# Decode attention: PV with p as an 8-column stationary and V moving 512 columns wide

## The chip, the core and the metric

One core of a Trainium2 chip runs the whole program. The metric is the device time in microseconds (us), median of several executions. All runs quoted below are undisturbed (fast). A ratio of two kernels is the mean time of one kernel's fast runs over that of the other's of the same rounds, so it is not quite the ratio of the medians that stand beside it; the interval with it is a 95% interval.

PE is the matmul engine, PEld its weight loads, DVE the vector engine, ACT the scalar engine, POOL a further engine that is all but idle here (2.4 us busy in before), SP the engine that issues the transfers. PSUM, in the code and the text, is where PE's results stand: the tiles `fold`, `otps`, `stps`, `qwps` and `yps` of the kernels, called banks here. The granted clock is the clock that PE was allowed, as a share of full speed, as the profile records it.

## The reference

Two independent halves, A and B, each a decode step of attention with one query token, 32 heads, 8192 cached tokens, head size 128, all bf16:

```
q = (x @ wq) per head                       # x: 1 x 512
scores = q . k_cache * 128**-0.5            # 32 heads x 8192
p = softmax(scores)
o = p @ v_cache                             # 32 heads x 128
y = concat(o) @ wo                          # 4096 x 512
```

K and V of both halves are 268 MB; everything else is small. The work is a long stream of transfers with little arithmetic on each byte.

## The kernel before

Heads are taken in pairs, 32 pairs over both halves. One pair's K, or V, is one 4 MB transfer into one of five slots of a ring, laid out with 64 partitions for each of the two heads and 128 tokens in each partition. For a pair j the engines do this:

- DVE multiplies K by q in place, in eight products M0 to M7.
- PE "folds" each half of the products over the head dimension: 16 matmuls against the identity, each moving 512 columns (fold 0 for M0 to M3, fold 1 for M4 to M7). DVE reduces the rest (R).
- The softmax goes over all engines: maxima on DVE (m1), a transpose on PE (tr), a maximum (m2), a broadcast on PE (bc), the exponents on ACT, their sum on PE (sum), the reciprocal on DVE (ri).
- PV multiplies p with V on PE. DVE scales the result into `ot` (o).

The parts that the change touches, with cuts marked by dots:

```python
def plan_PV(j):
    last = (j == NPR - 1)
    if not last:
        landed('PE', ('v', j))
    W('PE', c_e, e_val[j])                  # wait for the exponents
    if j >= 2:
        W('PE', c_o, o_val[j - 2])          # the PSUM bank is free
    t = kv(('v', j))
    ...
    def op(e, t0, t1):                      # TP = 128 tokens a partition
        for i in range(t0, t1):
            m = e.matmul(ot_ps[j % 2][:, 0:2], t[:, i, :], p2[:, j % 2, i, :],
                         start=(i == 0), stop=(i == TP - 1))
    ...
for j in range(NPR):                        # NPR = 32 pairs; c is j >= 1
    for i in range(4):
        plan_M(j, i)
    if j >= 2:
        plan_o(j - 2)
    if c:
        plan_R(j - 1, 1)
    plan_fold(j, 0)
    plan_M(j, 4)
    if c:
        plan_m1(j - 1)
        plan_tr(j - 1)
    plan_M(j, 5)
    if c:
        plan_m2(j - 1)
        plan_bc(j - 1)
        plan_exp(j - 1)
        plan_sum(j - 1)
    plan_M(j, 6)
    plan_M(j, 7)
    if c:
        plan_ri(j - 1)
    plan_fold(j, 1)
    plan_R(j, 0)
    if j < NPR - 1:
        if c:
            plan_PV(j - 1)
        if j == PPA + 1: ...plan_w(0, ...)  # half A: o rearranged for wo
        if j == PPA + 2: ...plan_y(0, ...)  # half A: y = o @ wo, 128 matmuls
        plan_w_ready(j - 2)                 # half B: o rearranged, in three blocks
...                                         # tail: the last pair, its PVs, y of B
```

Each engine runs its own list in the order in which these functions append to it. So in every pair PE does fold 0 of pair j, the small softmax products of pair j-1, fold 1 of pair j, PV of pair j-1.

In PV before, a 128x128 block of V is the stationary operand (a weight load) and the two columns of p move through it. For each of the 128 tokens of a partition there is one load and one 2-column matmul.

## Time and profile before

| | before |
|---|---|
| time, median of 3 | 683.4 us |
| span in the profile | 680.7 us |
| DMA | 90% or more in 39 of 40 slices, about 430 GB/s |
| mean granted PE clock | 0.79 |
| one pair, first fold matmul to the next pair's | 19.4 us in most pairs |

From the page: rows of the span in 40 slices (granted PE clock in tenths, mean busy share of the DMA engines in tenths, GB/s), then the chain of work that ended last by engine, then the costliest groups (busy us, mean ns of one, idle time before them and what ended it).

```profile
span 680.7 us, 12357 instructions
PEclk9998867877876867789867786967887668678885
DMA  9999999999999999999999999999999999999993
DMA 53%; PE 30%; DVE 12%; issue 3%; ACT 1%; ACTq 0%; DVEq 0%
L374 PE MATMUL fold<-ring,ident 128*128 128x512 bf16 x1024 | 320.5, 484 | 109.7 <-DVE ring L361 109.2
L361 DVE TENSOR_TENSOR ring<-ring,qbc 128x2048 bf16<-128x2048 bf16 x256 | 300.9, 1216 | 148.5 <-DMA ring<-in_A_k_cache_dram 84.9
L459 PE MATMUL otps<-p,ring 128*128 128x2 bf16 x4096 | 108.3, 163 | 1.5 <-issue 1.5
```

The transfers bound the kernel. Before its products DVE is idle 148 us in sum, waiting for K to land, and PE is idle because DVE is. The 8 MB of a pair at 430 GB/s take 19.5 us, and that is the pair's time.

From the timeline, PE's side of one early pair (start us, duration us, engine, line, operation; the row-sum product at 75.10 ends the softmax):

```profile
69.34 3.61 PE L374 MATMUL fold<-ring,ident 128*128 128x512 bf16 x16
72.79 0.27 PE L405 MATMUL stps<-ident_f,m 128*2 128x128 f32 x1
73.43 0.38 PE L415 MATMUL stps<-m,sel 2*128 2x1 f32 x2 [0.37 <-DVE m L410]
75.10 0.57 PE L436 MATMUL stps<-rowsum,ones_f 128*128 128x2 f32 x2 [1.29 <-ACT p L429]
75.70 5.02 PE L374 MATMUL fold<-ring,ident 128*128 128x512 bf16 x16
```

Here a fold takes 3.6 us or 5.0 us for the same 16 matmuls (in other pairs up to 6.6 us), 217 ns or up to 427 ns each. The granted clock is 1.00 over the first, 0.71 over the second and 0.54 over a fold of 6.6 us. Between the folds lies a gap of 2.8 us, in which PE waits for DVE and ACT. PV follows fold 1. The chain of waits (start us, us, what) has it at 3.21 us:

```profile
75.70 5.02 PE fold L374 x16
80.72 3.21 PE otps L459 x128
83.95 37.84 DMA ring<-in_A_k_cache_dram
```

3.21 us over 128 matmuls is 25 ns apiece, each with its own 128-column weight load; those of the last PVs, at a granted clock of 0.50, took 27 ns. The line at 83.95 is a K transfer that the end of PV let start, since it freed a slot of the ring. Three other transfers are still ahead of it and one lands every 9.7 us, so the rate of the transfers, and not the end of PV, sets when it lands, 37.84 us later.

### The profile page before, as it was taken

How to read it: one execution, taken by the hardware profiler on the slowest of the kernel's cores; microseconds unless marked ns; L12 is line 12 of the kernel's file. 1: busy time of each engine (PE TensorE's matmuls, PEld its weight loads, DVE VectorE, ACT ScalarE, POOL GpSimd, SP SyncE). 2: the span in 40 equal slices, each digit the busy share in tenths (PEclk: the TensorE clock that was granted, in tenths of full speed). 3: DMA queues.
4: the chain of work that ended last, by engine and by line, in shares of the span. 5: the costliest groups of instructions: out<-in, count | busy, mean ns of one | idle time of the engine just before them, and what ended most of it. 6: DMA issues, size and time to landing. Idle time of an engine off the chain costs nothing.

```text
span 680.7 us, 12357 instructions
## 1 busy us (share of the span) xinstructions
PE 479.8 (70%) x5660; PEld 264.9 (39%) x5660; DVE 377.8 (56%) x513; ACT 42.5 (6%) x169; POOL 2.4 (0%) x16
## 2 busy tenths in 40 slices
PE   0487877767688767856777576857768768667775
PEld 0133533434343434433433352534434234334445
DVE  4158556655555665555556526656555557463650
ACT  0110000000000000000000000000000001000000
POOL 1000000000000000000000000000000000000000
PEclk9998867877876867789867786967887668678885
DMA  9999999999999999999999999999999999999993
GB/s 370 431 430 431 431 433 429 429 430 430 427 435 433 428 430 432 430 426 430 431 430 429 431 430 430 428 405 432 429 432 432 428 426 430 430 430 433 422 415 131
DMA packets 11684, 286.01 MB, mean 420 GB/s; under 512 B 1776, under 2 KB 2288, under 8 KB 2672
## 3 DMA queue, kind: packets, MB, share of 16 engines
q1 hardware_dynamic: 11344, 285.22, 97.9%
q8 instruction: 44, 0.72, 0.4%
q14 instruction: 8, 0.07, 0.0%
q10 hardware_dynamic: 288, 0.00, 0.0%
HBM read 285.21 MB, written 0.00 MB: 419 GB/s over the span
## 4 chain that ended last, share of the span: by engine, by line
DMA 53%; PE 30%; DVE 12%; issue 3%; ACT 1%; ACTq 0%; DVEq 0%
DMA ring<-in_B_k_cache_dram 27%; DMA ring<-in_A_k_cache_dram 22%; PE fold L374 19%; DVE ring L361 11%; PE otps L459 7%; DMA xT<-in_B_x_dram 3%; PE qwps L333 2%; PE yps L537 1%; ACT qbc L340 1%; DVE m L410 1%; ACT p L429 0%; PE stps L436 0%; PE stps L405 0%; DVE wt L504 0%; PE stps L415 0%
## 5 line engine op out<-in xcount | busy, mean ns | idle before, releaser
L374 PE MATMUL fold<-ring,ident 128*128 128x512 bf16 x1024 | 320.5, 484 | 109.7 <-DVE ring L361 109.2
L361 DVE TENSOR_TENSOR ring<-ring,qbc 128x2048 bf16<-128x2048 bf16 x256 | 300.9, 1216 | 148.5 <-DMA ring<-in_A_k_cache_dram 84.9
L374 PEld LDWEIGHTS fold<-ring,ident 128*128 128x128 bf16 x1024 | 117.3, 120 | 287.8 <-issue 117.5
L459 PEld LDWEIGHTS otps<-p,ring 128*128 128x128 bf16 x4096 | 108.3, 97 | 8.7 <-issue 1.6
L459 PE MATMUL otps<-p,ring 128*128 128x2 bf16 x4096 | 108.3, 163 | 1.5 <-issue 1.5
L387 DVE TENSOR_REDUCE s_sb<-fold 128x64 f32<-128x512 f32 x64 | 43.1, 674 | 10.7 <-PE fold L374 10.3
L410 DVE TENSOR_REDUCE m<-stps 2x1 f32<-2x128 f32 x32 | 8.9, 279 | 69.8 <-PE stps L405 69.8
L436 PE MATMUL stps<-rowsum,ones_f 128*128 128x2 f32 x64 | 13.6, 282 | 41.5 <-ACT p L429 41.5
L421 ACT COPY nb<-stps 128x1 f32<-128x1 f32 x32 | 5.1, 159 | 580.3 <-PE stps L415 580.3
L333 PE MATMUL qwps<-ring,xsel 128*128 128x512 bf16 x64 | 16.7, 408 | 29.2 <-DVE xsel L226 24.3
L429 ACT ACTIVATE p<-s_sb,nb 64x128 bf16<-64x128 f32 x64 | 27.9, 436 | 2.1 <-ACT nb L421 0.3
L436 PEld LDWEIGHTS stps<-rowsum,ones_f 128*128 128x128 f32 x64 | 10.8, 211 | 44.2 <-ACT p L429 44.2
L333 PEld LDWEIGHTS qwps<-ring,xsel 128*128 128x128 bf16 x64 | 6.0, 103 | 39.4 <-issue 27.2
L415 PE MATMUL stps<-m,sel 2*128 2x1 f32 x64 | 12.3, 259 | 11.5 <-DVE m L410 11.5
L415 PEld LDWEIGHTS stps<-m,sel 2*128 2x128 f32 x64 | 9.6, 186 | 24.0 <-DVE m L410 24.0
L397 DVE TENSOR_REDUCE m<-s_sb 64x1 f32<-64x128 f32 x64 | 17.7, 277 | 1.0
L504 DVE TENSOR_TENSOR wt<-qwps,hmask 128x512 f32<-128x512 f32 (+3 forms) x5 | 2.2, 440 | 24.6 <-PE qwps L497 24.5
L429 ACT ACTIVATION_READ_ACCUMULATOR p<-s_sb,nb 64x1 f32 x64 | 11.7, 182 | 0.0
L475 DVE TENSOR_TENSOR ot<-otps,rinv 128x2 bf16<-128x2 f32 x32 | 4.9, 154 | 11.8 <-PE otps L459 11.8
L537 PE MATMUL yps<-w_bf,ring 128*128 128x1 bf16 x240 | 8.7, 172 | 1.9 <-issue 1.9
L537 PEld LDWEIGHTS yps<-w_bf,ring 128*128 128x128 bf16 x240 | 8.6, 118 | 1.9 <-issue 1.9
L405 PE MATMUL stps<-ident_f,m 128*2 128x128 f32 x32 | 8.8, 275 | 0.0
(30 smaller groups left out, 34.4 us busy)
## 6 DMA issues: line engine op xcount, KB each, us to landing
ring<-in_A_k_cache_dram SPq DMA_DIRECT2D x16, 4096.0 KB, 37.1
ring<-in_A_v_cache_dram SPq DMA_DIRECT2D x16, 4096.0 KB, 31.0
ring<-in_B_k_cache_dram SPq DMA_DIRECT2D x16, 4096.0 KB, 37.8
ring<-in_B_v_cache_dram SPq DMA_DIRECT2D x15, 4096.0 KB, 31.9
ring<-in_A_wq_dram SPq DMA_DIRECT2D x1, 4096.0 KB, 12.5
ring<-in_B_wq_dram SPq DMA_DIRECT2D x1, 4096.0 KB, 21.9
ring<-in_A_wo_dram SPq DMA_DIRECT2D x1, 4096.0 KB, 36.5
ring<-in_B_wo_dram SPq DMA_DIRECT2D x1, 2048.0 KB, 20.2
```

Of the source, the lines that this page charges most:

```text
L333: m = e.matmul(qw_ps[:, :].rearrange("p (j d) -> p j d", d=Dh), xsel[:, a, c, par, :], wq[:, c, 4 * g:4 * g + 4, par, :], start=(i == 0), ...
L361: m_val[(j, i)] = INC('DVE', c_m, lambda e: e.tensor_tensor(t, t, qbc[:, a, jj:jj + 1, :].broadcast_to([P, CH, Dh]), ALU.mult))
L374: m = e.matmul(fold_ps[h][:, :].rearrange("p (t e) -> p t e", e=FE), ident[:], t[:, h * HT:(h + 1) * HT, c * FE:(c + 1) * FE], start=(c == ...
L387: r_val[(j, h)] = INC('DVE', c_r, lambda e: e.tensor_reduce(s_sb[:, j % 2, h * HT:(h + 1) * HT], fold_ps[h][:, :].rearrange("p (t e) -> p ...
L397: m1_val[j] = INC('DVE', c_m1, lambda e, h=h, q0=q0, q1=q1: e.tensor_reduce(m1[q0:q1, j % 2, h:h + 1], s_sb[q0:q1, j % 2, :], AX.X, ALU.max))
L405: tr_val[j] = INC('PE', c_tr, lambda e: e.transpose(st_ps[j % 2][0:2, 0:P], m1[:, j % 2, :], ident_f[:]))
L410: m2_val[j] = INC('DVE', c_m2, lambda e: e.tensor_reduce(m2[0:2, j % 2:j % 2 + 1], st_ps[j % 2][0:2, 0:P], AX.X, ALU.max))
L415: bc_val[j] = INC('PE', c_bc, lambda e: e.matmul(st_ps[j % 2][:, P:P + 1], sel2[:], m2[0:2, j % 2:j % 2 + 1], start=True, stop=True))
L429: e_val[j] = INC('ACT', c_e, lambda e, h=h, q0=q0, q1=q1: e.activation(p2[q0:q1, j % 2, :, h], s_sb[q0:q1, j % 2, :], AF.Exp, bias=nb[q0:q ...
L436: s_val[j] = INC('PE', c_s, lambda e: e.matmul(st_ps[j % 2][:, P + 2:P + 4], ones_f[:], rowsum[:, j % 2, :], start=True, stop=True))
L459: m = e.matmul(ot_ps[j % 2][:, 0:2], t[:, i, :], p2[:, j % 2, i, :], start=(i == 0), stop=(i == TP - 1))
L537: m = e.matmul(y_ps[:, b:b + 1], wo[:, h0 + i, :, b], src[:, a, h0 + i:h0 + i + 1], start=(first and i == 0 and b == 0), stop=(lastblk and ...
```

## The change

The intent: the 4096 weight loads of PV look wasteful, each 128 columns for two columns of output. The change turns the product round. Four tokens of p for both heads are an 8-column stationary, and V moves through it, four tokens times 128 values, 512 columns wide: 32 matmuls a pair instead of 128. The result is an 8x512 block of which only the four 2x128 "diagonal" blocks (token with its own token) are wanted. ACT copies the block out of PSUM, and four small fp32 matmuls add the diagonal blocks and turn them back into two columns. The last two pairs keep the old PV.

The core of the diff; further lines make the tile `o8`, two semaphores, a wait of the transpose on the output multiply, and let PV wait for ACT's copy where it waited for the output multiply:

```diff
+            def wide(e):
+                for i in range(0, TP, TB):
+                    m = e.matmul(ot_ps[j % 2][0:2 * TB, :],
+                                 p2[:, j % 2, i:i + TB, :].rearrange("p t h -> p (t h)"),
+                                 t[:, i:i + TB, :].rearrange("p t d -> p (t d)"),
+                                 start=(i == 0), stop=(i == TP - TB))
+                m.then_inc(c_pv.sem, 1)
+            if j < NWIDE:
+                OP('PE', wide)
 ...
+                cp_val[j] = INC('ACT', c_cp, lambda e: e.copy(
+                    o8[:, j % 2, :], ot_ps[j % 2][0:2 * TB, :]))
 ...
+        def plan_ot(j):
+            W('PE', c_cp, cp_val[j])
+            W('PE', c_ri, ri_val[j])
+            v = ot_val[j] = c_ot.bump()
+
+            def op(e):
+                for i in range(TB):
+                    m = e.matmul(st_ps[j % 2][:, OC:OC + 2], o8[:, j % 2, i * Dh:(i + 1) * Dh],
+                                 ident_f[0:2 * TB, 2 * i:2 * i + 2],
+                                 start=(i == 0), stop=(i == TB - 1))
+                m.then_inc(c_ot.sem, 1)
+            OP('PE', op)
 ...
             for i in range(4):
                 plan_M(j, i)
-            if j >= 2:
-                plan_o(j - 2)
             if c:
                 plan_R(j - 1, 1)
             plan_fold(j, 0)
+            if j >= 2:
+                plan_ot(j - 2)
             plan_M(j, 4)
+            if j >= 2:
+                plan_o(j - 2)
             if c:
                 plan_m1(j - 1)
                 plan_tr(j - 1)
```

The fp32 products stand behind fold 0 on PE, and the output multiply that waits for them stands ahead of the maxima on DVE.

## The prediction

> **What bounds it now.** The page shows the DMA engines 90% or more busy in 39 of 40 slices at about 430 GB/s. A pair of heads brings 8 MB of K and V, so a pair costs 19.5 us of transfer; 32 pairs, wq and wo fill the span of 680.7 us. DMA leads the chain of waits (53%). PE is not far behind. From the timeline, one pair costs PE: fold 0 (16 matmuls 128x512, 3.5 us at full clock, 5.0 to 5.3 at half), a gap of 2.8 us for maximum, exponent and sum, fold 1 (3.6 to 5.3), and PV, 128 loads with 2-wide matmuls in 3.2 to 3.4 us at either clock. That is 13 to 17 us: PV is hidden.
>
> **What the change does.**
> 1. PV becomes 32 matmuls, each streaming 512 columns. The fold takes 217 ns each at full clock and 427 ns at half: estimate 6.9 us, or up to 13.7, for 3.3 us. PE gains +3.6 us a pair at best.
> 2. New: one ACT copy 8x512, about 0.6 us, hidden under fold 0; four fp32 matmuls with 128-column loads. The row-sum product shows two loads of 0.15 us, so about 1.2 us.
> 3. Order. The output multiply on DVE now comes after those fp32 matmuls, which come after fold 0, ahead of the maximum and of product 5. Now they follow serially: fp32 1.2, multiply 0.2, two maxima 0.6, product 5 1.2, then 2.6 as before to fold 1. PE's gap in a pair grows from 2.8 to about 5.8 us.
>
> **The new pair.** 3.5 + 5.8 + 3.5 + 6.9 = 19.7 us at full clock throughout: no slack against 19.5. [...] the clock records here show just 0.5 and 1.0, in multiples of 3.41 us. In this trace a window followed by full clock had about 6.5 or more 512-wide matmuls (40% of it streaming), and narrow PV hardly counted. A gap of 5.8 us always contains a window under that, so fold 1 starts at half clock and loses 1 to 2.5 us. Wide PV should count as activity, so it and fold 0 run warm. I estimate 20.5 to 22.5 us a pair, about 21.7: this loop bounds, DMA waits for slots.
>
> **Sum.** Fold 0 of pair 2 starts at 69.3 us, about 73 after. 29 pairs at 21.7 = 629; wo work of half A, now exposed, about 10; the tail from the last fold 0, about 32 as now (last two PVs unchanged); 2 us from span to time. I say 744.
>
> **Time: 744 us, 8 in 10 within 712 to 775. Faster by over 2%: 0.02; within 2%: 0.06; slower: 0.92.**
>
> **What would show it.** DMA busy digits drop to 8, rate near 385 GB/s; "DVE waits for K" nearly gone; chain mostly PE fold and PV instead of DMA; fold 0 near 217 ns a matmul, fold 1 partly 427; PV 6.9 us; mean clock up to about 0.85; fold starts 20.5 to 22.5 us apart.
>
> **What would make it wrong.** If an 8-column stationary does not count as activity, PV runs at half clock: 27 us a pair, over 880 us. If the gap is near 4.5 us, or the windows lock favourably (six are 20.48 us), about 710. If the fp32 matmuls overlap well, it stays DMA-bound, within 2%.

The sum: 73 + 629 + 10 + 32 + 2 = 746, stated as 744.

## The result, and the profile after

The changed kernel takes 777.1 us (775.6 to 781.3, four runs), before 683.3 us (682.4 to 684.3, four runs). The ratio is 1.138 (1.134 to 1.143). The direction and nearly all of the mechanism were as predicted; the time lies 2 us above the range and 33 us above the point.

The same lines of the page of after:

```profile
span 775.3 us, 7136 instructions
PEclk9999988988988988889988787988998869988786
DMA  9999999999999989899989598999998959989540
PE 77%; DVE 13%; ACT 4%; DMA 3%; issue 2%; DVEq 0%; ACTq 0%
L376 PE MATMUL fold<-ring,ident 128*128 128x512 bf16 x1024 | 303.0, 463 | 24.3 <-DVE ring L363 23.9
L363 DVE TENSOR_TENSOR ring<-ring,qbc 128x2048 bf16<-128x2048 bf16 x256 | 300.6, 1215 | 10.2 <-DMA ring<-in_A_k_cache_dram 9.2
L479 PE MATMUL otps<-ring,p 128*8 128x512 bf16 x960 | 212.1, 379 | 0.0
L525 DVE TENSOR_TENSOR ot<-stps,rinv 128x2 bf16<-128x2 f32 x30 | 4.8, 160 | 272.4 <-PE stps L510 272.4
```

DMA fell from 53% of the chain to 3%, and PE rose from 30% to 77%. DVE no longer waits for K (10 us in sum instead of 148). It waits 272 us for the fp32 products, 9 us in each pair. PE, with the steps of DVE and ACT between its two folds, has become the loop that everything else waits for. The mean clock rose to 0.86: wide PV runs at a granted clock of 1.00 in every pair (219 ns a matmul), and the regular fold 0 behind it takes 3.6 us where before has 5.6 us in the mean.

PE's side of one regular pair in the timeline of after (the four fp32 products show as x8):

```profile
312.99 3.63 PE L376 MATMUL fold<-ring,ident 128*128 128x512 bf16 x16
316.55 1.05 PE L510 MATMUL stps<-ident_f,o 8*128 8x2 f32 x8
318.42 0.27 PE L408 MATMUL stps<-ident_f,m 128*2 128x128 f32 x1 [0.82 <-DVE m L399]
319.87 0.38 PE L418 MATMUL stps<-m,sel 2*128 2x1 f32 x2 [1.18 <-DVE m L413]
321.54 0.59 PE L439 MATMUL stps<-rowsum,ones_f 128*128 128x2 f32 x2 [1.29 <-ACT p L432]
322.14 6.58 PE L376 MATMUL fold<-ring,ident 128*128 128x512 bf16 x16
```

And the chain of waits goes on from there without a wait for anybody but PE:

```profile
322.14 6.58 PE fold L376 x16
328.72 7.00 PE otps L479 x32
335.72 3.56 PE fold L376 x16
```

This pair is 3.6 (fold 0) + 5.5 (gap) + 6.6 (fold 1, here almost all at half clock) + 7.0 (PV). Over the regular pairs the mean is 21.81 us, with fold 1 at 5.7 us in the mean. PV's 32 matmuls at 219 ns cost 7.00 us where 128 small ones cost 3.21: the loads that the change removed had been cheaper than the columns that it moves.

The granted clock of fold 1 can be followed in time. The table below cuts the timeline of after into stretches of 3.4 us (for each engine busy us and number of instructions; then the granted clock, the DMA share, GB/s):

```profile
314.50:317.90 3.40, 3.10 (x18) 1.75 (x16) 0.19 (x2) 0.00 (x0) 0.00 (x0) 1.00 1.07 463
317.90:321.30 3.40, 0.65 (x3) 0.37 (x3) 3.34 (x6) 0.96 (x4) 0.00 (x0) 1.00 0.98 424
321.30:324.80 3.50, 3.25 (x9) 1.49 (x10) 3.42 (x5) 0.18 (x2) 0.00 (x0) 0.51 0.84 365
324.80:328.20 3.40, 3.40 (x10) 1.16 (x9) 2.67 (x3) 0.00 (x0) 0.00 (x0) 0.51 0.65 280
328.20:331.60 3.40, 3.40 (x17) 1.25 (x16) 1.82 (x2) 0.00 (x0) 0.00 (x0) 1.00 0.56 154
```

The second stretch lies in the gap; PE is busy 0.65 us of it, and the clock is halved in the third (0.51). The third has about six matmuls of fold 1 at half clock, and the fourth is halved too (0.51). The clock records of before and after hold only 0.5 and 1.0, and all but the last of each trace's entries (92 and 72) last 3.41 us or a whole multiple of it. "Window" below means one such 3.41 us of the record.

### The profile page after: what moved, and what is told of

Read it like the earlier page. It is cut to its first block, busy times and chain, and to the rows that moved or that the text cites. A ratio compares the mean times of both kernels' runs of the same rounds, so it can differ in the third digit from the quotient of the medians.

```text
span 775.3 us, 7136 instructions
## 1 busy us (share of the span) xinstructions
PE 614.3 (79%) x3020; PEld 274.8 (35%) x3020; DVE 379.0 (49%) x513; ACT 59.7 (8%) x199; POOL 2.4 (0%) x16
## 4 chain that ended last, share of the span: by engine, by line
PE 77%; DVE 13%; ACT 4%; DMA 3%; issue 2%; DVEq 0%; ACTq 0%
PE fold L376 38%; PE otps L479 27%; DVE ring L363 9%; PE stps L510 4%; DMA xT<-in_B_x_dram 3%; ACT p L432 3%; PE qwps L335 2%; PE stps L439 2%; DVE m L399 2%; PE stps L418 2%; PE yps L587 1%; PE otps L472 1%; DVE m L413 1%; DVE ot L525 1%; ACT nb L424 1%
## 5 line engine op out<-in xcount | busy, mean ns | idle before, releaser
L376 PE MATMUL fold<-ring,ident 128*128 128x512 bf16 x1024 | 303.0, 463 | 24.3 <-DVE ring L363 23.9
L363 DVE TENSOR_TENSOR ring<-ring,qbc 128x2048 bf16<-128x2048 bf16 x256 | 300.6, 1215 | 10.2 <-DMA ring<-in_A_k_cache_dram 9.2
L479 PE MATMUL otps<-ring,p 128*8 128x512 bf16 x960 | 212.1, 379 | 0.0
L376 PEld LDWEIGHTS fold<-ring,ident 128*128 128x128 bf16 x1024 | 112.9, 115 | 198.2 <-issue 106.0
L525 DVE TENSOR_TENSOR ot<-stps,rinv 128x2 bf16<-128x2 f32 x30 | 4.8, 160 | 272.4 <-PE stps L510 272.4
L479 PEld LDWEIGHTS otps<-ring,p 128*8 128x8 bf16 x960 | 81.0, 87 | 128.7 <-issue 12.7
L439 PE MATMUL stps<-rowsum,ones_f 128*128 128x2 f32 x64 | 18.2, 354 | 41.2 <-ACT p L432 41.2
L490 ACT COPY o<-otps 8x512 f32<-8x512 f32 x30 | 17.2, 574 | 398.5 <-PE otps L479 398.5
L510 PEld LDWEIGHTS stps<-ident_f,o 8*128 8x128 f32 x240 | 28.9, 186 | 12.7 <-issue 12.7
L510 PE MATMUL stps<-ident_f,o 8*128 8x2 f32 x240 | 31.4, 249 | 0.0
L439 PEld LDWEIGHTS stps<-rowsum,ones_f 128*128 128x128 f32 x64 | 15.4, 299 | 44.0 <-ACT p L432 44.0
```

The lines of the kernel that those rows point to most:

```text
L363: m_val[(j, i)] = INC('DVE', c_m, lambda e: e.tensor_tensor(t, t, qbc[:, a, jj:jj + 1, :].broadcast_to([P, CH, Dh]), ALU.mult))
L376: m = e.matmul(fold_ps[h][:, :].rearrange("p (t e) -> p t e", e=FE), ident[:], t[:, h * HT:(h + 1) * HT, c * FE:(c + 1) * FE], start=(c == ...
L439: s_val[j] = INC('PE', c_s, lambda e: e.matmul(st_ps[j % 2][:, P + 2:P + 4], ones_f[:], rowsum[:, j % 2, :], start=True, stop=True))
L479: m = e.matmul(ot_ps[j % 2][0:2 * TB, :], p2[:, j % 2, i:i + TB, :].rearrange("p t h -> p (t h)"), t[:, i:i + TB, :].rearrange("p t d -> p ...
L490: cp_val[j] = INC('ACT', c_cp, lambda e: e.copy(o8[:, j % 2, :], ot_ps[j % 2][0:2 * TB, :]))
L510: m = e.matmul(st_ps[j % 2][:, OC:OC + 2], o8[:, j % 2, i * Dh:(i + 1) * Dh], ident_f[0:2 * TB, 2 * i:2 * i + 2], start=(i == 0), stop=(i ...
```

## The experiments

The theory to test: four costs add up. (1) Wide PV is 3.8 us longer. (2) The fp32 products and the output multiply stand in a serial chain from fold 0 to fold 1 and lengthen the gap by 2.7 us. (3) The longer gap puts fold 1 at half clock. (4) With the slack of PE gone, the wo work, which was absorbed before, is paid in full. Rival A: the streaming of wide PV alone makes the loss, order is harmless. Rival B: the V slots are held longer and the transfers starve. Rival C: the serial part alone makes the loss.

"Extra of the wo pairs" below is the time of the seven pairs with wo work (pairs 17 to 19, 25, 26, 29, 30, counted from 0) less seven times the mean of the 21 regular pairs from pair 3 on, all taken from the starts of fold 0 in the timeline of the profiled run. Where the transfers set the pace, the pairs after a stall catch up, and the last two columns do not separate cleanly (e2, e5, e6 and e9, whose regular pairs are under the 19.4 us of most pairs of before).

| kernel | time us | before, same rounds | ratio (95%) | regular pair us | gap us | extra of wo pairs us |
|---|---|---|---|---|---|---|
| before | 683.3 | | | 19.58 | 2.8 | 12.6 |
| after | 777.1 | 683.3 | 1.138 (1.134–1.143) | 21.81 | 5.5 | 36.5 |
| e1_o_late | 711.6 | 685.7 | 1.038 (1.037–1.040) | 19.52 | 3.8 | 39.1 |
| e2_ot_late | 697.8 | 685.7 | 1.017 (1.015–1.020) | 19.16 | 2.8 | 37.5 |
| e3_heat | 716.0 | 685.7 | 1.045 (1.043–1.047) | 19.70 | 5.5 | 36.0 |
| e4_w_first | 750.4 | 685.7 | 1.096 (1.092–1.100) | 21.82 | 5.5 | 10.4 |
| e5_narrow_serial | 687.3 | 683.8 | 1.004 (1.002–1.007) | 19.08 | 5.3 | 26.1 |
| e6_ot_late_w_first | 680.3 | 683.8 | 0.995 (0.992–0.997) | 19.35 | 2.8 | 11.5 |
| e7_heat_w_first | 691.9 | 683.8 | 1.012 (1.009–1.015) | 19.70 | 5.5 | 9.2 |
| e8_before_w_first | 684.3 | 684.3 | 0.999 (0.997–1.002) | 19.60 | 2.8 | 11.6 |
| e9_e6_again | 679.5 | 684.3 | 0.993 (0.991–0.995) | 19.31 | 2.8 | 14.9 |
| e10_fetch | 695.4 | 683.7 | 1.017 (1.014–1.019) | 19.88 | 2.8 | 12.9 |

All ten gave correct results.

### e1_o_late: only the output multiply moved

```diff
             plan_M(j, 4)
-            if j >= 2:
-                plan_o(j - 2)
 ...
             if c:
                 plan_ri(j - 1)
+            if j >= 2:
+                plan_o(j - 2)
             plan_fold(j, 1)
```

> After, with only the DVE output multiply moved: it stands behind product 7 instead of ahead of the two maxima; the fp32 products stay right behind fold 0. My theory (a serial loop of PE and DVE, plus the clock windows): the gap between fold 0 and fold 1 falls from 5.5 to about 3.9 us (2.8 plus 1.05 of the fp32 products), a regular pair from 21.75 to about 20.5 us, the time from 777 to about 741 us. Rival A (only the streaming of the wide PV costs; order is harmless): stays at 777. Rival B (DMA starves because the V slot is held longer): stays at 777.

Measured: 711.6 us, from 777. The gap fell to 3.8 us as expected, but the pair fell more than expected, to 19.5 instead of 20.5 us. The reason is the clock: with this gap fold 1 is at full clock in some pairs (3.6 us) and partly or mostly at half clock in others (5.3 to 6.4 us), so its mean fell from 5.7 to 5.1 us (mean granted clock of the run 0.89 against 0.857). With the 1.7 us of the gap that makes the 2.3 us. Moving one 0.16 us instruction took 65 us off. It left wide PV and the slots untouched, so rivals A and B fall as the whole cause.

### e2_ot_late: the fp32 products moved as well

```diff
             plan_fold(j, 0)
-            if j >= 2:
-                plan_ot(j - 2)
 ...
             plan_fold(j, 1)
+            if j >= 2:
+                plan_ot(j - 2)
             plan_R(j, 0)
+            if j >= 2:
+                plan_o(j - 2)
```

(The output multiply is taken from where after has it.)

> After, with the fp32 products moved behind fold 1, just ahead of PV, and the output multiply behind the fold's reduction: PV is still wide. My theory: the gap is 2.8 us again as before, the PE loop costs 3.6 + 2.8 + 3.6 to 5.3 + 1.05 + 6.95 = 18.0 to 19.7 us, about the 19.45 us of the transfers, so the time is 685 to 705 us, of which the wo work of both halves may leave some. Rival A (wide PV alone costs it): well above 740.

Measured: 697.8 us, inside the range. PV is as wide as in after, and the products take the same 1.05 us, but now ahead of PV, in the stretch where PE is dense. The gap is that of before, and the regular pairs are near the pace of the transfers. Of the 94 us lost, 79 came back by order alone, with no less work.

### e3_heat: the clock by itself

```diff
+        def plan_heat(j, n):
+            if 2 <= j < NPR - 1:
+                ...
+                        e.matmul(ot_ps[(j - 1) % 2][:, :], ident[:],
+                                 selw[16][:, 0:4, :].rearrange("p t d -> p (t d)"),
+                                 start=True, stop=True)     # n times
 ...   # n = 3 behind the fp32 products, 4 behind tr, 5 behind bc
```

The results of these matmuls are never read.

> After, with 12 dummy bf16 matmuls 128x512 a pair put into the gap where PE waits (3, 4 and 5), writing a bank that PV starts anew: nothing else moved. If the half clock of fold 1 is a cost of its own: clock record near 1.0 through the regular pairs, fold 1 3.6 us instead of 4.9 to 6.6, gap unchanged at 5.5, a pair about 19.5 us instead of 21.75, time about 712 us. If the clock does not matter (the loop is bound elsewhere, or dummies delay the chain): 777 or more.

Measured: 716.0 us (expected about 712). PE's side of one pair in its timeline, then the clock row of its page:

```profile
116.25 1.05 PE L510 MATMUL stps<-ident_f,o 8*128 8x2 f32 x8
117.46 0.59 PE L632 MATMUL otps<-selw,ident 128*128 128x512 bf16 x2 [0.16 <-issue]
118.23 1.02 PE L632 MATMUL otps<-selw,ident 128*128 128x512 bf16 x4
119.87 1.25 PE L632 MATMUL otps<-selw,ident 128*128 128x512 bf16 x5
121.83 3.63 PE L376 MATMUL fold<-ring,ident 128*128 128x512 bf16 x16 [0.22 <-DVE ring L363]
125.39 7.07 PE L479 MATMUL otps<-ring,p 128*8 128x512 bf16 x32
```

```profile
PEclk9999999999999999999999879999999989999986
```

(One dummy of the first three is missing from this record, as in every pair; its weight load is there.) The gap is still 5.5 us, but the mean granted clock is 0.964, fold 1 is 3.63 us in every regular pair, and the pair is 19.70 us. So 61 us of the loss pass through the half clock of fold 1, and useless work in idle time bought them back. These 61 us and the 65 of e1 are not two separate shares of the 94: e1 also gains by the clock, and under some 19.5 us a pair the transfers take over.

### e4_w_first: where the wo work stands

```diff
             if j < NPR - 1:
-                if c:
-                    plan_PV(j - 1)
                 if j == PPA + 1: ...
                 if j == PPA + 2: ...
                 plan_w_ready(j - 2)
+                if c:
+                    plan_PV(j - 1)
```

> After, with the permutation matmuls of wo and the y matmuls of half A planned ahead of PV of their pair instead of behind it, so that DVE makes the next pair's products during PV. In after, seven pairs (17 to 19, 25, 26, 29, 30) took 37 us more than the regular 21.75 each; the prediction had 10. My theory: that work stood with PE idle, because DVE's share of it and then four products (4.6 us) came between PV and the next fold 0. Expected: about 12 us left of the 37, time about 752 us, regular pairs unchanged. Rival (the extra is PE work or wo's transfer): 770 or more.

Measured: 750.4 us (the profiled run, 755.8 us, was the slowest of the four), and the extra of the wo pairs fell from 36.5 to 10.4 us with the regular pairs unchanged. This was the term that the prediction had too small. In after, PE and DVE in the first wo pair (timeline, PE then DVE) show what happened:

```profile
422.22 0.57 PE L547 MATMUL qwps<-ot,selw 128*128 128x32 bf16 x16
423.64 0.57 PE L547 MATMUL qwps<-ot,selw 128*128 128x32 bf16 x16 [0.86 <-DVE wt L554]
430.42 1.89 PE L376 MATMUL fold<-ring,ident 128*128 128x512 bf16 x4 [6.21 <-DVE ring L363]
```

```profile
422.89 0.69 DVE L554 TENSOR_TENSOR wt<-qwps,hmask 128x512 f32<-128x512 f32 x1 [12.03 <-PE qwps L547]
425.74 4.62 DVE L363 TENSOR_TENSOR ring<-ring,qbc 128x2048 bf16<-128x2048 bf16 x4
```

The rearranging matmuls themselves take 1.1 us. But DVE's part of them stands in its list ahead of the next pair's products, and waits 12 us for PE, all through PV. Only then does it make the four products (4.6 us) that fold 0 needs, with PE idle for 6.2 us. In the other pairs DVE makes these products during PV.

### e5_narrow_serial: the serial part without the wide PV

```diff
-                OP('PE', wide)
+                OP('PE', lambda e: op(e, 0, TP))
 ...
-                    m = e.matmul(st_ps[j % 2][:, OC:OC + 2], o8[:, j % 2, i * Dh:(i + 1) * Dh],
-                                 ident_f[0:2 * TB, 2 * i:2 * i + 2],
-                                 start=(i == 0), stop=(i == TB - 1))
+                    m = e.matmul(st_ps[j % 2][:, OC:OC + 2], ident_f[:], o8[:, j % 2, :],
+                                 start=True, stop=True)
```

(`o8` holds the two result columns here; each of the four products writes the right value.)

> After, with PV narrow again (128 loads of V, 2-wide moving) in all pairs, but the rest of the change kept: an ACT copy of the PV result, four fp32 products with 128-column loads behind fold 0 (each yields the same right value), the output multiply behind them and ahead of the maxima. So the serial part of the change without the wide PV. My theory: the gap is about 5.5 us, both folds are mostly at half clock, a pair costs PE 5.0 to 5.5 + 5.5 + 5 + 3.4, about 19 to 20.5 us, about the transfers' 19.45: time 684 to 715 us, far from the 777 of after. Rival A (wide PV alone costs it): as before, within 1%. Rival C (the serial part alone costs it): above 745.

Measured: 687.3 us, 0.4% over before. Rival C falls. This run does not tell my theory from rival A, since both allowed this time; e1, e2 and e6 do that. Together with e6 it makes the point: the long gap alone costs 0.4%, wide PV in a good order costs nothing, and both together, as in after, cost 14%. Each fits into PE's slack, the sum does not.

### e6_ot_late_w_first: both orders mended

This is e2 and e4 together.

> e2_ot_late (697.8) together with e4_w_first: PV is wide, the fp32 products stand in the dense stretch ahead of PV, the output multiply off the chain, and the wo work ahead of PV. In e2 the seven pairs with wo work still took 28 us more than their neighbours. My theory: most of that goes, and the kernel is bound by the transfers again: 684 to 690 us, within 1% of before and not faster, because before was bound by the same transfers. Rival (wide PV has a cost of its own that order does not cure): 694 or more.

Measured: 680.3 us, below the expected 684 to 690, and 0.5% faster than before where "not faster" was expected, with an interval clear of 1. DVE waits for the transfers again, 66.6 us in sum where after had 10:

```profile
L363 DVE TENSOR_TENSOR ring<-ring,qbc 128x2048 bf16<-128x2048 bf16 x256 | 300.8, 1216 | 66.6 <-DMA ring<-in_B_k_cache_dram 44.5
```

So wide PV has no cost that order does not cure, and the loss of after is accounted for.

### e7_heat_w_first: do the two costs add?

This is e3 and e4 together.

> e3_heat (716.0) together with e4_w_first (750.4): the dummies keep the clock up and the wo work stands ahead of PV; the order of fp32 products and output multiply is that of after. If the two costs are separate and add: 777 less 61 less 27, about 690 us, the regular pair 19.7 us, the seven pairs with wo work about 10 us over it in sum. If they are one and the same idle time seen twice: 705 or more.

Measured: 691.9 us against about 690 expected, with the pair at 19.70 us and the extra at 9.2 us. The clock's 61 us and the wo work's 26 us are separate and add.

### e8_before_w_first and e9_e6_again: whence the last half per cent?

e8 is the reordering of e4 applied to the kernel before; e9 is the kernel of e6 again, in the same rounds.

> Before, with narrow PV in all pairs, and only the wo work planned ahead of PV as in e4. e6_ot_late_w_first was 0.5% faster than before (680.3 against 683.8). If that small gain comes of the wo work's place (fewer stalls in pairs 17, 18, 25, 29, transfers fed better), this kernel has it too: about 680. If it comes of the wide PV (a V slot freed differently, folds at full clock), this kernel is as before, 683 to 684.

> The kernel of e6_ot_late_w_first once more, in the same rounds as e8_before_w_first, for a comparison of the two on one chip: 679 to 682 again.

Measured: e8 684.3 us, the same as before (0.999); e9 679.5 us, 0.7% faster than before. So the gain of e6 does not come of the wo work's place alone.

### e10_fetch: more instructions on an idle engine

```diff
+            W('POOL', c_f, f_val[(j, 0)])
+            W('POOL', c_pad, c_pad.n)
+            for i in range(128):
+                INC('POOL', c_pad, lambda e, i=i: e.memset(pad[0:1, i:i + 1], 0.0))
             plan_fold(j, 1)
```

> The kernel of e6 and e9 plus 128 one-element memsets a pair on the otherwise idle POOL (4096 in all), which touch nothing that others use. Question: why e6 and e9 are 0.5 to 0.7% faster than before. In before the instruction queue moved 44 packets of 16 KB for PE (about 1.07 us each on one DMA engine), in e9 24, since 4096 loads and as many matmuls became 960 each. Theory: fewer instructions leave the DMA engines to the data. Then this kernel, with 4096 more instructions (about 16 packets' worth), gives back half or more of the gain: 681 to 683, ratio to before 0.996 to 1.0. Rival (the gain comes of PE's steady full clock and earlier slots): stays at 679 to 680, ratio 0.993. Void if DVE's products get longer than 1.22 us by POOL's writes.

Measured: 695.4 us, 15.9 us more than e9, and 15.1 us more than e6, which is the same kernel as e9 measured on the chip of this run. The direction is that of the theory, the size far above it. DVE's products were not slower (1216 ns against 1215), so the run is not void. The queues of the two kernels (packets, MB, share), e9 first:

```profile
q8 instruction: 24, 0.39, 0.2%
q14 instruction: 8, 0.07, 0.0%
```

```profile
q8 instruction: 24, 0.39, 0.2%
q14 instruction: 40, 0.33, 0.1%
```

In total 0.26 MB more moved, a tenth of a per cent of the data. The end of e10 shows how that can cost 2%. These are stretches of its last 24 us (the last two columns are the mean busy share of the 16 DMA engines, and GB/s):

```profile
667.00:670.00 3.00, 1.94 (x9) 0.99 (x10) 2.05 (x4) 0.76 (x4) 3.00 (x92) 0.92 0.37 152
670.00:673.00 3.00, 3.00 (x9) 1.07 (x8) 0.00 (x0) 0.00 (x0) 0.02 (x1) 0.51 0.08 33
676.00:679.00 3.00, 3.00 (x79) 2.93 (x76) 0.63 (x3) 0.00 (x0) 0.00 (x0) 0.56 0.09 33
682.00:685.00 3.00, 3.00 (x114) 2.94 (x111) 0.00 (x0) 0.00 (x0) 0.00 (x0) 0.50 0.09 33
```

For 15 us the share lies between 0.05 and 0.09; one engine of 16 is 0.06. The packed trace lists every packet with its start and duration, though not its engine, and there the data packets after 671.5 us run one after another without overlap, as if one engine still worked off its share; the last V lands at their end, at 685.6 us.

The packets also show why. An added packet takes 0.31 us, during which 15 data packets run and not 16, and the data packet behind it takes 1.57 us instead of 1.215. If packets are matched end to start (within 5 ns, an inference), the 32 added ones lie on only four chains, in runs of 9, 9, 2 and 12: they fell on one engine at a time. A pair is 256 data packets of 32 KB, 16 for each engine if they are spread evenly, and 16 x 1.215 = 19.4 us. With one added packet and the delay behind it that is 20.1 us, and e10's regular pairs have a median of 20.08 us. By this estimate the slowest engine set the pace. Whether the memsets disturbed anything else was not tested apart, but this delay alone accounts for the pair.

Before has 44 packets of 16 KB on the instruction queue q8 where e9 has 24, and its last V lands at 674.9 us (e8: 674.5) where e6 and e9 have 671.0 and 671.8. These packets take 1.07 us each and lengthen the next by about 0.5 us, but, matched in the same way, they are spread over the engines. An estimate from that, 20 packets x 1.55 us / 16, is 1.9 us, about half of the 3.5 to 4.8 us gained. No run isolates it, and the rest of the half per cent stays open.

## Why the prediction was wrong in its size

The prediction was a sum. Term by term:

| term | predicted us | measured us |
|---|---|---|
| start of fold 0 of pair 2 | 73 | 73.5 |
| 29 pairs at the regular pace | 29 x 21.7 = 629 | 29 x 21.81 = 632.5 |
| wo work | 10 | 36.5 |
| from the last fold 0 to the end | 32 | 33.5 |
| span to time | 2 | 1.8 |
| sum | 746, stated as 744 | 777.8 (time 777.1; pair 2 is 0.5 under the mean) |

- **What bounds it before**: right. Transfers at 430 GB/s.
- **Wide PV 6.9 us instead of 3.3, with it and fold 0 at full clock**: right. 7.00 us, and the granted clock is 1.00 over PV and over fold 0 in the regular pairs.
- **The gap grows from 2.8 to about 5.8 us**: right in mechanism; 5.5, since the fp32 products took 1.0 and not 1.2.
- **Fold 1 falls to half clock and loses 1 to 2.5 us**: right. 5.7 us in the mean instead of 3.6, a loss of 2.1, at a granted clock of 0.53 to 0.72; e3 shows it by itself.
- **The pair at 20.5 to 22.5, about 21.7 us**: right. 21.81.
- **What would show it**: waits for K nearly gone (10 us), clock up to about 0.85 (0.857). DMA rate near 385 GB/s was 368, for the reason that follows.
- **The step that failed**: "wo work of half A, now exposed, about 10". It measured 36.5 us. There are two mistakes in it. First, half B's work was left out: two of its three blocks are rearranged within the loop as well, and pairs 25, 26, 29 and 30 show 15.8 us for them. Second, half A's was too small. The prediction does not say where its 10 came from; on the chain of before this work adds up to 9.6 us, so it was probably taken from there. In pairs 17 to 19 of after it cost 20.7 us. PE's own matmuls for it are 5.5 us of this (1.1 to rearrange, 4.4 for y). The rest arises because the next pair's products stand behind it on DVE and PE idles meanwhile (6.2 and 4.8 us), and because fold 0 then starts at half clock (5.4 and 6.4 us instead of 3.6 in pairs 18 and 19, at a granted clock of 0.66 and 0.55). e4 takes 26 us of the 36.5 away by order alone. These stalls existed in before too: after pair 17's fold 1 PE needed 11.2 us to the next fold 0. There the transfers had run ahead, and the next pairs caught up, so the sum of those pairs was 12.6 us over the mean, most of it probably the 4 MB of half A's wo itself (its transfer took 9.7 us).

With the right term the sum would have been 744 plus 27, or 771, inside the range.

## What to carry to other kernels

When a change moves the bound from transfers to a loop of engines, cost again everything that the old bound used to hide, also work that the change does not touch; here that was 27 of the 33 us of error. Place an operation by what waits behind it: the same wide PV cost 14% with its small products on the serial chain and nothing with them in the dense stretch. And a weight load that moves two columns may be the cheaper form: 128 small matmuls at 25 ns beat 32 wide ones at 219 ns.

## What the clock records of before and after show

- With the 512-column matmuls counted from their recorded starts, all windows at full clock in which these took under 0.30 of the time were followed by half clock, and all in which they took over 0.40 by full clock; between the two, either followed. Of the windows at half clock, all under 0.77 were followed by half clock and all over 0.78 by full clock. The count is rough, since some matmul records are missing.
- A gap of 2.8 us was enough in part of the pairs. In before the window from 71.74 to 75.15 us, with most of the gap that begins at 72.95 us in it, had a share of 0.31, the next was at half clock, and fold 1 took 5.02 us. Behind a gap of the same length fold 1 took 3.63 us in 10 of the 21 regular pairs and 4.98 to 5.31 us in the other 11.
- Narrow matmuls hardly counted. PV before fills PE's row with loads and 2-column matmuls for 3.3 us a pair, yet seven windows at full clock with 0.67 to 0.76 of PV and 0.24 to 0.33 of fold were followed by half clock. In after all 27 windows filled by wide PV (8-column stationary, 512 moving columns) were followed by full clock.
